# A recorded delta-rule kernel: loads of v and r on SyncE, transfers on fewer DMA engines, and other DMA costs in the planner of its order

## The chip, the core and the metric

The kernel runs on one core of a Trainium2 chip, with its five engines: TensorE (PE, whose weight loads the profile shows as PEld), VectorE (DVE), ScalarE (ACT), GpSimd (POOL) and SyncE (SP), and 16 DMA engines. Time is the device time of one execution in microseconds (us); the median of the runs is what is compared.

## The reference, cut to what matters

```python
def _attn_ref(r, k, v, w, a, b):            # each 4 x 8 x 768 x 40
    state = zeros((B, H, D, D))
    for t in range(S):
        y[:, :, t] = einsum('bhd,bhde->bhe', rt, state)
        Sa = einsum('bhde,bhe->bhd', state, at)
        state = state * wt[:, :, None, :] - einsum('bhd,bhe->bhde', Sa, bt)
        state = state + einsum('bhd,bhe->bhde', vt, kt)
    return y

def _moe_ref(x, w_skip, w_gate, w1, w2):    # x: 3072 x 320
    do_compute = x @ w_skip > 0
    xc = x[do_compute]
    e_idx = argmax(xc @ w_gate, axis=1)     # 8 experts, gate: softmax at e_idx
    for e in range(E):
        y[e_idx == e] = gate_w * (relu(xc[e_idx == e] @ w1[e]) @ w2[e])
    out[do_compute] = xc + y                # other rows: out = x
```

The first part is a recurrence over 768 steps for 32 heads with a decay w, a removal along a and b, and an added outer product of v and k. The second sends each of its 3072 rows with a positive skip score through one of 8 experts.

## The kernel before, in words

The 768 steps are cut into 24 chunks c of 32 steps; two chunks make a pair h of 64. The 32 heads lie in two halves x of 16. For each pair, VectorE turns the decay into running products (scan_z, scan_d, scan_w, on the tiles Z, D and Wx), kbm and l1a scale k, b and a by them, and m1 multiplies on TensorE to two matrices per head: one goes by ScalarE into AB, the other is transposed by VectorE, masked, and copied in four small transfers (32 rows of 256 numbers) into rows of L1. tinv inverts the triangular matrices of two pairs, step by step on VectorE (tinv0 for the first two pairs, in blocks of 16), into TB. kbt transposes k and b into L2, wex and wtt the decay into WT, m2 multiplies v by r and puts the result in R1.

Then each chunk goes through a chain: rs and ux multiply the state and the chunk's rows (R1) by L1, uq multiplies that by TB, GpSimd masks a part of it, sst makes the next state and yy the output, which VectorE scales into XS. SyncE stores XS to the output; route finds the expert of each row, and GpSimd scatters the rows by an indirect DMA into xg, which has been filled with padding (pad). When the chunks are done, experts runs the 8 experts over xg, with weights split into a high and a low part; load(e) brings the raw weights of expert e into WR, which holds KB and L1 of the first part until then.

The loads of the first part are: load_w (decay), load_kb (k and b), load_a (a), load_v (v as rows, 32 rows), load_rv (v, 64 or 128 rows, tiles vvt, SCR and one of rrt), load_rr (r, tiles rrt), l1z (zeros) and the identity rows idl. The first pairs are loaded in one piece of 104 or 128 rows, later ones in two pieces of 40 rows (cutl). Each takes the queue of the engine that issues it, in order: SyncE for most, and GpSimd for load_rv and load_rr behind the first chunk. In the built program, a transfer of SyncE also waits for the one that stands eight places ahead of it.

The order of all that is not the order of the code. Until chunk 22, the object Rec records every instruction as a task with its reads and writes. Rec.plan then goes through the tasks with costs for each engine (cost), for a transfer (pipe), for waits between engines (HOP, EX) and for TensorE's instruction stream (256 instructions to a block, a block at least BLK us), and takes on each engine the task with the smallest key, or a later one that is done within LET us of the other's start. flush issues the tasks in the order of their planned starts (line 272 in the profile). What stands behind chunk 22's flush keeps the order of the code (line 134). So a change of a cost moves instructions on all engines.

Of the kernel before, what the change touches and what calls it, by code (L numbers as in the profile page):

```python
# [15 lines left out]
DRAM = bass.MemoryType.DRAM  # L16
B,H,S,D=4,8,768,40
# [45 lines left out]
class Rec:  # L63
# [1 line left out]

    ENG=dict(vector='V',scalar='A',gpsimd='G',tensor='P',sync='S')
    HOP={'PA':0.066,'VA':0.034,'AV':0.033,'PV':0.11,'AP':0.053,'VP':0.055,'GP':0.054,'AG':0.08,'VG':0.13,'PG':0.17}
    EX=dict(V=0.08,P=0.07,A=0.0,G=0.0,S=0.0); PW=1.25; BLK=3.6; SLOW=0.8; BW=2.7e5; DSC=0.012; AHEAD=2.5
    def hop(s,e,f): return (0.114 if e=='V' else 0.0) if e==f else s.EX[e]+s.HOP.get(e+f,0.04)
    def __init__(s,nc):  # L70
        s.nc=nc; s.on=False; s.ni=0; s.tasks=[]; s.own={}; s.na=0; s.first={}; s.cache={}; s.banks={}; s.rest=()
# [28 lines left out]
    def cost(s,e,op,w,r,a):  # L100
        sz=lambda x: int(np.prod([d[1] for d in list(x.ap)[1:]])) if len(list(x.ap))>1 else 1
        n=max(sz(x) for x in (w[:1]+r[:1]))
        if 'dma' in op: return (1.06,2.6) if 'ind' in op else (0.63 if e=='S' else 0.55,2.2)
        ps=any('PSUM' in str(x.space).upper() for x in r)
        if e=='P':
            o=sz(w[0]); m=w[0].ap[0][1]
            if op=='transpose': return max(0.145,0.04+0.001*o),0
            if m<16: return 0.05+0.0016*o,0
            if m==16: return 0.022,0
            if m==32: return 0.034 if o<16 else 0.0098+0.00041*o,0  # L110
            if m<=48: return 0.0213+0.00072*o,0
            if m<=64: return max(0.072,0.028+0.00075*o),0
            return max(0.11,0.0021*o),0
        if e=='A': return 0.15+0.00085*n+(0.06+0.07*(n>99) if op=='activation' else 0.12 if abs(w[0].ap[-1][0])>8 and n>99 else 0.0),0
        if e=='G': return (0.08+n*0.0008 if op=='memset' else 0.18 if op=='tensor_copy' else 0.2+0.00195*n),0
        if op=='tensor_tensor_scan': return 0.02+0.00217*n,0
        if op=='transpose': return 0.08+0.00115*n*(1 if n<1000 else 1.6),0
        if op=='memset': return 0.04+0.0003*n,0
        if op=='reciprocal': return 0.17,0
        if op=='tensor_tensor': return (0.1 if ps and 'PSUM' not in str(w[0].space).upper() and n>199 else 0.06)+0.00105*n*(1 if ps or n<99 else 1.75),0  # L120
        return 0.12+0.00105*n,0
    def pipe(s,w,r):

        n=int(np.prod([d[1] for d in w.ap])); run=n
        for x in (w,r):
            q=1
            for st,k in reversed(list(x.ap)[0 if 'DRAM' in str(x.space).upper() else 1:]):
                if k>1 and st!=q: break
                q*=k
            run=min(run,q)  # L130
        p=w if 'DRAM' not in str(w.space).upper() else r
        return 4*n/min(6e5,5e3*max(16,p.ap[0][1]))+n/run*s.DSC/16
    def call(s,e,op,fn,a,k):
        if not s.on: return fn(*a,**k)  # L134
        def ap(x):
# [48 lines left out]
    def plan(s,keep=None):  # L184
# [33 lines left out]
        while done<N:  # L218
            best=None
            for e in 'VAGPS':  # L220
                c=[]
                for i in pool[e] if not keep else [i for i in pool[e] if i==seq[e][nxt[e]]]:
                    w=want(i) if T[i].al else (0.0,None)
# [15 lines left out]
            if e=='P':  # L239
                pos+=t.k  # L240
                while pos>=256*(blk+1):
                    x=max(fin[i],ent+s.BLK); fin[i]=x; ent=x; blk+=1
            if t.L and e in 'VG': port[e]=fin[i]
            free[e]=fin[i]; [pool[f].remove(i) for f in pool if i in pool[f]]; done+=1; nxt[e]+=1
            lat=t.lat
            if t.f==1: gi=fin[i]+s.IND
            elif e=='G' and t.f==2: gi=-1.0
            if t.x: dq=max(dq,fin[i]+1.0)+t.x; lat=max(lat+t.x,dq+1.2-fin[i])
            for j in t.n:
                rdy[j]=max(rdy[j],fin[i]+lat+s.hop(e,T[j].e)+(s.IHOP if T[j].f==1 and e=='V' else 0.0)); left[j]-=1  # L250
                if not left[j]: put(j)
# [2 lines left out]
                if not users[o]:  # L254
                    at[bank[o]]=last[o]
        s.st,s.fin,s.bank_of,s.en,s.span=st,fin,bank,en,max(fin)
    LET=0.7; FAR=1.0; ALT=1.0; FILL=None
    def keys(s):

        w=max(sum(t.d for t in s.tasks if t.e==e) for e in 'VAGP')/len(s.tasks)  # L260
# [44 lines left out]
def attn(ctx,tc,i,m,out,X):  # L305
# [10 lines left out]
    V,A,G,TE,SP=nc.vector,nc.scalar,nc.gpsimd,nc.tensor,nc.sync  # L316
# [32 lines left out]
    def load_kb(h):  # L349
        if h>=NH: return  # L350
        H[h]['KB']=KBa[h%4]; cutl(SP,H[h]['KB'],i['kb'][h],h<4,NK(h))
    def load_a(h,dst=None):
        if h>=NH: return
        H[h]['a']=a_.rearrange("p (u t) -> p u t",u=16) if dst is None else dst; cutl(SP,H[h]['a'],i['at'][h],h<5,PR)
    RR=[cp.tile([128,1024],F32,name=f"rrt{q}") for q in range(2)]; VV=[cp.tile([128,1024],F32,name="vvt"),SCR[:,0:1024]]
    rvt={}
    def load_rv(c,E=G):
        if c>=NC: return
        t=VV[0] if c%2==0 else RR[1] if c==1 else VV[1]
        rvt[c]=t.rearrange("p (u t) -> p u t",u=16); cutl(E,rvt[c],i['vv'][c],c<4,128)  # L360
    rrt={}
    def load_rr(h,E=G):

        if h>=NH: return
        rrt[h]=RR[h%2].rearrange("p (u t) -> p u t",u=16); cutl(E,rrt[h],i['rr'][h],h<2,128)
    def load_v(c,x):
        if c>=NC: return
        SP.dma_start(R1[x][c%NR1][ao[x]:ao[x]+32,:,0:40],i['vt'][c,x])
    def scan_z(h,dst=None,E=None,rv=rv):
        if h>=NH: return  # L370
        E=E or SE
# [32 lines left out]
        E.tensor_tensor(H[h]['KB'][0:NR(h),:,:,q,:],H[h]['KB'][0:NR(h),:,:,q,:],v4(Wi)[0:NR(h)],ALU.mult)  # L404
    def l1z(h,x):
        if h>=NH: return
        SP.dma_start(L1[x][h%NL][ao[x]:ao[x]+32].rearrange('p u c t -> p (u c t)'),i['zer'][0:32,0:1024])
    def l1a(h,x,E=None):
        if h>=NH: return
        E=E or G  # L410
# [208 lines left out]
    if 1:  # L619

        with tc.manual_schedule(engines={ET.Pool}):
# [15 lines left out]
            wchk(0,0); wchk(0,1)  # L637
            for x in range(2): zero(fR(x,0))
            for x in range(2): load_v(0,x)
            load_rv(0,SP); load_rr(0,SP); load_kb(2)  # L640
            scan_z(0,None,V); scan_d(0); scan_w(0,V); load_w(2)
            kbm(0,1); kbm(0,0,V); l1a(0,0,V); scan_z(1,alt[:,1041:2083],V); l1a(0,1,V)
            scan_d(1); scan_w(1,V)
# [4 lines left out]
            for x in range(2):  # L648
                for c in range(2): m1(0,x,c,V)
            for x in range(2): l1a(1,x,V)  # L650
            load_a(2,L1t[:,3072:4096].rearrange("p (u t) -> p u t",u=16)); load_rv(1,SP)
            for b in range(4): kbt(0,b)
            wchk(1,0); wchk(1,1)
            scan_z(2,None,V); scan_d(2); scan_w(2,V)
# [2 lines left out]
                for c in range(2): m1(1,x,c)  # L657
            for x in range(2): m2(0,x)
            for x in range(2):
                for c in range(2): SP.dma_start(L2[x][0][64*x:64*x+64,c],i['idl'][x,64*x:64*x+64])  # L660
            load_kb(3); load_w(3,alt[:,0:1041]); load_a(3,a1)
            t0=tinv0(Xi); next(t0)
            def Tb(k):
# [24 lines left out]
            load_a(4)  # L688
            wchk(3,0); wchk(3,1)
            for x in range(2):  # L690
                for c in range(2): SP.dma_start(L2[x][1][64*x:64*x+64,c],i['idl'][x,64*x:64*x+64])
        tg=iter(()); tn=[0]
        def T(k=1):
            tn[0]+=1
# [12 lines left out]
        for c in range(NC):  # L707
# [91 lines left out]
            if j==2: wex(2*ph+2,0)  # L799
            if c: m2(c+1,1)  # L800
            T()
            load_rv(c+2,G if c else SP)
            if c%2 or c==0: load_rr((c+3)//2,G if c else SP)
            if c<2: m.pad(2*c); m.pad(2*c+1)
            if c==22: m.load(1)
            RP('3c')
# [40 lines left out]
class Moe:  # L847
# [10 lines left out]
        s.base=s.base0; s.WH,s.WL={},{}  # L858
    def consts(s): s.nc.sync.dma_start(s.mc,s.i['mc']); s.nc.sync.dma_start(s.wg,s.i['wg'])
    def pad(s,k):  # L860
        s.nc.sync.dma_start(s.xg.rearrange("(q p) d -> p q d",p=128)[:,4*k:4*k+4],s.i['xpad'].unsqueeze(1).broadcast_to([128,4,XW]))
    def xpose(s,X):
        nc=s.nc
        pt=s.ps.tile([128,3,128],F32,tag="pp",name="ptx")
# [79 lines left out]
    def load(s,e):  # L944
        if e>=E_: return
        SP=s.nc.sync; r=s.raw[e%2]
        for k in range(2): SP.dma_start(r[:,1024*k:1024*k+1024],s.i['w1'][e,128*k:128*k+128])
        for k in range(2): SP.dma_start(r[64*k:64*k+64,2048:3072],s.i['w1'][e,256:320])
        for k in range(2): SP.dma_start(r[:,3072+1280*k:4352+1280*k].rearrange("p (k d) -> p k d",k=4),s.i['w2'][e,512*k:512*k+512].rearrange("(k p) d -> p k d",p=128))
    def base_last(s):  # L950
        s.nc.vector.tensor_copy(s.base1,s.base); s.base=s.base1
    def split(s,e,wp=None):
# [188 lines left out]
```

## Time and profile before

| | us |
|---|---|
| median of 3 runs (lowest, highest) | 624.01 (620.74, 625.52) |
| the profiled execution | 625.9 |
| its span, first to last instruction | 624.0 |
| busy in the span: PE, DVE, ACT, POOL | 470.0, 472.7, 390.0, 315.5 |
| mean granted clock of TensorE | 0.923 |

The span is what the trace covers; the profiled execution took 1.9 us more. Busy times are averages over stages of different kinds, so they are read by stretch. The DMA engines moved 80.59 MB, 129 GB/s over the span.

### The profile page before, as it was taken

Reading aid. Unit: us, or ns where it says so; the run is one execution under the profiler, and the core shown is the slowest. Engines: PE = TensorE matmul, PEld = TensorE weight load, DVE = VectorE, ACT = ScalarE, POOL = GpSimd, SP = SyncE. Lnnn points to the kernel's source line nnn. Section 1 sums busy time; section 2 is a strip of 40 time slices with the busy share of each in tenths; the row PEclk is TensorE's granted clock in tenths of the full one; section 3 lists DMA queues with packets and bytes.
Section 4 is the critical chain, followed back from the end, with each engine's and each line's share of the span. In section 5 each row is a group of like instructions: output and inputs, shape, how many; then the busy total and the mean of one; then the engine's idle time right before and its main releaser. Section 6 shows DMA issues by size and latency. Waiting matters only on the chain. (4 is left out here: it accounts for less than half of the span.)

```text
span 624.0 us, 28751 instructions
## 1 busy us (share of the span) xinstructions
PE 470.0 (75%) x12424; PEld 407.5 (65%) x12424; DVE 472.7 (76%) x1269; ACT 390.0 (62%) x982; POOL 315.5 (51%) x285
## 2 busy tenths in 40 slices
PE   0154327877787887887887789878977999999992
PEld 0143216666666666776776677667765799999992
DVE  6525894789997987998989879865783558898860
ACT  7073216878695877887696769577865455555510
POOL 4133626437491868477583853234223266666751
PEclk9997757899897998998798989989988999999997
DMA  8997232433452453425351534453663477775100
GB/s 190 251 270 226 78 99 65 130 81 92 93 137 75 108 143 100 133 67 147 87 153 40 144 98 109 101 153 95 167 168 93 123 220 232 240 225 156 43 18 18
DMA packets 64360, 80.59 MB, mean 129 GB/s; under 512 B 33698, under 2 KB 52719, under 8 KB 63124
## 3 DMA queue, kind: packets, MB, share of 16 engines
q1 hardware_dynamic: 58323, 64.55, 38.6%
q0 software_dynamic: 5904, 14.15, 8.2%
q8 instruction: 99, 1.62, 1.2%
q14 instruction: 34, 0.27, 0.1%
HBM read 67.80 MB, written 13.15 MB: 130 GB/s over the span
## 5 line engine op out<-in xcount | busy, mean ns | idle before, releaser
L272 ACT COPY R1t<-pc 32x288 f32<-32x288 f32 (+4 forms) x254 | 98.8, 389 | 38.1 <-PE pc L272 32.4
L272 POOL TENSOR_TENSOR R1t<-R1t,mc 64x512 f32<-64x512 f32 x43 | 55.5, 1292 | 70.9 <-ACT R1t L272 64.7
L272 DVE TENSOR_TENSOR px<-px,M 128x168 f32<-128x168 f32 (+10 forms) x240 | 61.2, 265 | 2.3
L134 POOL TENSOR_TENSOR WL<-WR,WH 128x1280 fp32r<-128x1280 f32 (+1 forms) x21 | 57.8, 2794 | 8.6 <-ACT WH L134 8.6
L272 POOL TENSOR_TENSOR WR<-WR,M 104x1024 f32<-104x1024 f32 x19 | 41.6, 2207 | 35.5 <-DVE M L272 22.9
L272 DVE TENSOR_TENSOR M<-M,px 128x168 f32<-128x168 f32 (+10 forms) x240 | 54.4, 255 | 2.0 <-DVE px L272 0.2
L272 DVE TENSOR_TENSOR_SCAN M<-M 104x1041 f32<-104x1041 f32 (+1 forms) x20 | 47.0, 2348 | 0.2
L272 ACT COPY R1t<-pq 32x256 f32<-32x256 f32 (+4 forms) x101 | 36.2, 358 | 8.4 <-PE pq L272 5.3
L134 ACT CAST WH<-WR 128x1024 fp32r<-128x1024 f32 (+1 forms) x35 | 39.6, 1132 | 0.0
L272 POOL DMA_INDIRECT xg<-XS,ix x20 | 24.1, 1206 | 29.9 <-DMA xg<-XS,ix 11.7
L134 POOL DMA_INDIRECT out<-ro,ti x16 | 15.8, 989 | 44.3 <-DVE ro L134 10.7
L272 PE MATMUL pc<-UX,TB 32*32 32x104 f32 (+1 forms) x1024 | 30.2, 245 | 9.0 <-issue 7.9
L134 ACT ACTIVATE hH<-pc 128x512 fp32r<-128x512 f32 x21 | 12.6, 599 | 37.8 <-PE pc L134 37.8
L134 DVE CAST ti<-xe 128x2 int32<-128x2 f32 x8 | 35.0, 4376 | 0.2
L272 PE MATMUL py<-L2t,R1t 128*32 128x40 f32 x1344 | 23.4, 208 | 12.1 <-issue 9.4
L134 PE MATMUL pc<-xH,WH 128*128 128x256 f32 x126 | 32.5, 283 | 0.0
L272 DVE TENSOR_TENSOR R1t<-pc,D 40x512 f32<-40x512 f32 (+1 forms) x44 | 26.6, 605 | 6.3 <-PE pc L272 4.2
L134 DVE TENSOR_TENSOR WL<-WR,WH 128x1024 fp32r<-128x1024 f32 (+1 forms) x19 | 23.8, 1253 | 9.9 <-ACT WH L134 9.4
L272 ACT COPY R1t<-ps 40x288 f32<-40x288 f32 (+4 forms) x72 | 27.5, 383 | 5.4 <-PE ps L272 4.2
L272 PE MATMUL ps<-R1t,L2t 128*40 128x72 f32 (+1 forms) x672 | 28.6, 233 | 2.8 <-ACT R1t L272 1.6
L272 PEld LDWEIGHTS pc<-UX,TB 32*32 32x32 f32 x1024 | 21.5, 107 | 14.0 <-issue 10.1
L272 PEld LDWEIGHTS py<-L2t,R1t 128*32 128x32 f32 x1344 | 17.7, 114 | 16.3 <-issue 11.7
(353 smaller groups left out, 1537.0 us busy)
## 6 DMA issues: line engine op xcount, KB each, us to landing
WR<-w SPq DMA_DIRECT2D x16, 640.0 KB
WR<-w SPq DMA_DIRECT2D x16, 512.0 KB
WR<-kb SPq DMA_DIRECT2D x16, 320.0 KB
WR<-w SPq DMA_DIRECT2D x16, 256.0 KB
R1t<-vt SPq DMA_DIRECT2D x48, 80.0 KB
out<-XS SPq DMA_DIRECT2D x24, 160.0 KB
rrt<-rr POOLq DMA_DIRECT2D x20, 160.0 KB, 5.4
vvt<-vv POOLq DMA_DIRECT2D x20, 160.0 KB, 6.1
```

Source lines behind the costliest of these rows:

```text
L134: if not s.on: return fn(*a,**k)
L272: for fn,a,k,own in s.tasks[i].calls: (fn if s.en[i]==s.tasks[i].e else s.nc.vector.tensor_copy)(*[at(x,own) for x in a],**{n:at(x,own) fo ...
```

## The change

Three things change. All calls of load_rv and load_rr take SyncE's queue. The 32 rows of v, the zero rows, the identity rows, the padding of xg and the weights of experts 0 and 1 get an outermost dimension of 8 on the side of the memory, by which the transfer is shared out to 8 DMA engines; the weights of later experts get 16, as many as before. Loads of 40 rows, all on SyncE now, run on 10. And the planner has other costs: one pipe of 200 GB/s that transfers pass one after the other, 1.7 us to land, no fixed 2.2 us; a block of TensorE's instructions at 3.4 us; LET 1.2.

```diff
-    EX=dict(V=0.08,P=0.07,A=0.0,G=0.0,S=0.0); PW=1.25; BLK=3.6; SLOW=0.8; BW=2.7e5; DSC=0.012; AHEAD=2.5
+    EX=dict(V=0.08,P=0.07,A=0.0,G=0.0,S=0.0); PW=1.25; BLK=3.4; SLOW=0.0; BW=2.0e5; AHEAD=2.5; LAND=1.7
...
-        if 'dma' in op: return (1.06,2.6) if 'ind' in op else (0.63 if e=='S' else 0.55,2.2)
+        if 'dma' in op: return (1.06,2.6) if 'ind' in op else (0.63 if e=='S' else 0.55,0.0)
...
-        p=w if 'DRAM' not in str(w.space).upper() else r
-        return 4*n/min(6e5,5e3*max(16,p.ap[0][1]))+n/run*s.DSC/16
+        return max(4*n/s.BW,n/run*0.002)
...
-                    x=max(fin[i],ent+s.BLK); fin[i]=x; ent=x; blk+=1
+                    x=max(fin[i],ent+s.BLK+s.SLOW*min(8.0,max(0.0,dq-ent))); fin[i]=x; ent=x; blk+=1
...
-            if t.x: dq=max(dq,fin[i]+1.0)+t.x; lat=max(lat+t.x,dq+1.2-fin[i])
+            if t.x:
+                a=fin[i]+(0.5 if e=='S' else 1.5); b=max(dq,a); dq=b+t.x
+                if t.x<0.3: b=a+0.4*(b-a)
+                lat=b+t.x+s.LAND-fin[i]
...
-    LET=0.7; FAR=1.0; ALT=1.0; FILL=None
+    LET=1.2; FAR=1.0; ALT=1.0; FILL=None
...
-    def load_rv(c,E=G):
+    def load_rv(c,E=SP):
...
-    def load_rr(h,E=G):
+    def load_rr(h,E=SP):
...
-        SP.dma_start(R1[x][c%NR1][ao[x]:ao[x]+32,:,0:40],i['vt'][c,x])
+        SP.dma_start(R1[x][c%NR1][ao[x]:ao[x]+32,:,0:40],i['vt'][c,x].rearrange('(a b) u d -> a b u d',a=8))
...
-            load_rv(c+2,G if c else SP)
-            if c%2 or c==0: load_rr((c+3)//2,G if c else SP)
+            load_rv(c+2)
+            if c%2 or c==0: load_rr((c+3)//2)
...
+        n=8 if e<2 else 16
-        for k in range(2): SP.dma_start(r[:,1024*k:1024*k+1024],s.i['w1'][e,128*k:128*k+128])
+        for k in range(2): SP.dma_start(r[:,1024*k:1024*k+1024],s.i['w1'][e,128*k:128*k+128].rearrange('(a b) f -> a b f',a=n))
```

The new order differs from the first rows on. On TensorE, at the start of the program, rrt with vvt or with the other rrt is m2, WR with mc is kbt, WE with mc is wtt, and WR 32x64 is m1. Before:

```order
L272 MATMUL pq_99<-mc,WE_130 128x104 x4
L272 MATMUL pc_101<-rrt_118,vvt 64x64 x8
L272 MATMUL pq_99<-rrt_118,vvt 64x64 x8
L272 MATMUL pc_100<-mc,WE_130 128x104 x4
L272 MATMUL pq_99<-rrt_118,rrt_119 64x32 x8
L272 MATMUL pc_100<-rrt_118,rrt_119 64x32 x8
L272 MATMUL pc_101<-mc,WR 128x104 x4
L272 MATMUL pq_99<-mc,WR 128x104 x4
L272 MATMUL pc_100<-WR 32x64 x16
```

On TensorE, the same place in the new order:

```order
L274 MATMUL pq_99<-mc,WE_130 128x104 x4
L274 MATMUL pc_101<-mc,WR 128x104 x4
L274 MATMUL pc_100<-mc,WR 128x104 x4
L274 MATMUL pq_99<-WR 32x64 x16
L274 MATMUL pc_101<-WR 32x64 x16
L274 MATMUL ps_103<-WR 32x64 x16
L274 MATMUL pc_100<-WR 32x64 x16
L274 MATMUL ps_102<-mc,WR 128x104 x8
```

The four rows of m2 have moved behind kbt and m1 of the first pairs; the first of them now stands 14 rows further down.

On VectorE, behind the two scans of pair 0 (M<-M), the scans of pair 1 (L2t) and the copies of token numbers from mc into XS. Before:

```order
L272 SCALAR_TENSOR_TENSOR M<-M 104x1040
L272 COPY XS_149<-mc 128x2
L272 MEMSET M 128x17
L272 COPY XS_150<-mc 128x2
L272 SCALAR_TENSOR_TENSOR L2t<-L2t,M 104x1041
```

On VectorE, the same place in the new order:

```order
L274 SCALAR_TENSOR_TENSOR M<-M 104x1040
L274 MEMSET M 128x17
L274 SCALAR_TENSOR_TENSOR L2t<-L2t,M 104x1041
L274 TENSOR_SCALAR D_125<-L2t 104x16
L274 RECIPROCAL M<-D_125 104x16
```

The copies into XS have moved 28 rows down, into the first steps of the inverse.

On SyncE, in the middle of the program, a piece of the new order with the loads that GpSimd issued before (vvt, SCR and rrt):

```order
L274 DMA out<-XS_149 4x32x320
L274 DMA vvt<-vv 40x1024 x2
L274 DMA M<-at 40x1024
L274 DMA R1t<-vt 32x16x40 x2
L274 DMA out<-XS_149 4x32x320
L274 DMA SCR<-vv 40x1024 x2
L274 DMA rrt_119<-rr 40x1024
L274 DMA L1t<-zer 32x1024
L274 DMA rrt_119<-rr 40x1024
L274 DMA L1t<-M 32x256
```

The loads of v and r now stand between the other transfers of a chunk, with zero rows, v rows and the small copies of m1 behind them. At the start of SyncE's order, M<-wt of pair 2 has moved ahead of mc, and the four transfers of padding have moved from the 22nd to 28th row to the 34th to 47th.

## Rows read from the trace of the kernel before

**Rows 1.** Table of stretches: length, busy us by engine, TensorE clock, DMA share, GB/s.

```profile
0.00:20.00 20.00, 0.00 (x0) 0.00 (x0) 9.74 (x11) 12.03 (x16) 7.14 (x11) 1.00 0.87 193
20.00:40.00 20.00, 4.12 (x47) 3.45 (x48) 12.84 (x13) 6.36 (x16) 2.15 (x1) 1.00 0.94 263
40.00:60.00 20.00, 11.45 (x322) 9.89 (x320) 7.22 (x10) 11.58 (x38) 9.92 (x6) 0.84 0.89 262
60.00:100.00 40.00, 14.60 (x630) 12.31 (x631) 32.85 (x62) 9.81 (x29) 18.30 (x27) 0.59 0.29 82
100.00:490.00 390.00, 318.02 (x10501) 260.78 (x10497) 318.65 (x1068) 289.89 (x803) 204.34 (x204) 0.94 0.43 111
490.00:590.00 100.00, 99.94 (x775) 99.47 (x776) 78.86 (x92) 54.77 (x74) 60.99 (x30) 1.00 0.64 190
```

**Rows 2.** Chain that ended last, its first piece: start, length, what.

```profile
475.11 0.07 DVE XS L134
```

**Rows 3.** VectorE in order of time, 0 to 60 us; idle before in brackets.

```profile
9.39 2.32 DVE L272 TENSOR_TENSOR_SCAN M<-M 104x1040 f32<-104x1040 f32 x1
22.40 0.25 DVE L272 COPY XS<-mc 128x2 f32<-128x2 f32 x2 [10.68 <-DMA mc<-mc]
...
35.43 0.07 DVE L272 MEMSET M<- 128x17 f32 x1
46.49 0.32 DVE L272 STREAM_TRANSPOSE M<-pc 128x128 f32<-128x128 f32 x1 [10.99 <-ACT M L272]
...
53.12 0.24 DVE L272 RECIPROCAL M<-D 104x16 f32<-104x16 f32 x1
59.08 1.25 DVE L272 STREAM_TRANSPOSE M<-M 128x1024 f32<-128x1024 f32 x1 [5.72 <-ACT M L272]
```

**Rows 4.** TensorE in order of time, 0 to 60 us.

```profile
22.51 0.93 PE L272 MATMUL pq<-mc,WE 104*128 104x104 f32 x4 [22.51 <-DMA mc<-mc]
30.26 1.12 PE L272 MATMUL pc<-rrt,vvt 128*64 128x64 f32 x16 [6.83 <-DMA rrt<-rr]
...
39.66 1.07 PE L272 MATMUL pq<-rrt,rrt 128*64 128x32 f32 x16 [6.54 <-DMA rrt<-vv]
...
41.52 0.96 PE L272 MATMUL pc<-mc,WR 104*128 104x104 f32 x4
...
57.87 0.69 PE L272 MATMUL pc<-WR,M 128*32 128x64 f32 x17 [3.84 <-issue]
```

**Rows 5.** DMA issues: out, in, queue, count, size of each.

```profile
xg<-xpad SPq DMA_DIRECT2D x4, 644.0 KB
...
L2t<-idl SPq DMA_DIRECT2D x8, 160.0 KB
...
M<-wt SPq DMA_DIRECT2D x2, 422.9 KB
```

**Rows 6.** Instructions on tile vvt: ns min/median/max, first and last start.

```profile
L272 POOL DMA_DIRECT2D vvt<-vv x20: 507/554/607, 116.9 to 425.7; - x20
L272 SPq DMA_DIRECT2D vvt<-vv x2: 339/346/352, 7.9 to 39.6; - x2
```

**Rows 7.** Waits of GpSimd, 100 to 490 us: us in total, times, longest.

```profile
POOL SCR L272 <- PE pc L272: 9.1, 3, 4.1
...
POOL vvt L272 <- PE pc L272: 6.2, 3, 4.6
...
POOL SCR L272 <- PE pq L272: 4.6, 2, 3.6
```

**Rows 8.** Waits of TensorE, 100 to 490 us, those without a releaser.

```profile
PE pc L272 <- issue: 12.1, 13, 3.8
...
PE py L272 <- issue: 9.4, 8, 3.2
PE pq L272 <- issue: 4.2, 7, 1.4
```

**Rows 9.** DMA queues, 100 to 490 us: packets, MB, share of 16 engines.

```profile
q8 instruction: 82, 1.34, 1.6%
```

More of the change, by code (lines that the diff above doesn't have):

```diff
@@ L406, in l1z @@
         if h>=NH: return
-        SP.dma_start(L1[x][h%NL][ao[x]:ao[x]+32].rearrange('p u c t -> p (u c t)'),i['zer'][0:32,0:1024])
+        SP.dma_start(L1[x][h%NL][ao[x]:ao[x]+32].rearrange('p u c t -> p (u c t)'),i['zer'][0:32,0:1024].rearrange('(a b) f -> a b f',a=8))
     def l1a(h,x,E=None):
@@ L639, in attn @@
             for x in range(2): load_v(0,x)
-            load_rv(0,SP); load_rr(0,SP); load_kb(2)
+            load_rv(0); load_rr(0); load_kb(2)
             scan_z(0,None,V); scan_d(0); scan_w(0,V); load_w(2)
@@ L650, in attn @@
             for x in range(2): l1a(1,x,V)
-            load_a(2,L1t[:,3072:4096].rearrange("p (u t) -> p u t",u=16)); load_rv(1,SP)
+            load_a(2,L1t[:,3072:4096].rearrange("p (u t) -> p u t",u=16)); load_rv(1)
             for b in range(4): kbt(0,b)
@@ L659, in attn @@
             for x in range(2):
-                for c in range(2): SP.dma_start(L2[x][0][64*x:64*x+64,c],i['idl'][x,64*x:64*x+64])
+                for c in range(2): SP.dma_start(L2[x][0][64*x:64*x+64,c],i['idl'][x,64*x:64*x+64].rearrange('(a b) u d -> a b u d',a=8))
             load_kb(3); load_w(3,alt[:,0:1041]); load_a(3,a1)
@@ L690, in attn @@
             for x in range(2):
-                for c in range(2): SP.dma_start(L2[x][1][64*x:64*x+64,c],i['idl'][x,64*x:64*x+64])
+                for c in range(2): SP.dma_start(L2[x][1][64*x:64*x+64,c],i['idl'][x,64*x:64*x+64].rearrange('(a b) u d -> a b u d',a=8))
         tg=iter(()); tn=[0]
@@ L860, in pad @@
     def pad(s,k):
-        s.nc.sync.dma_start(s.xg.rearrange("(q p) d -> p q d",p=128)[:,4*k:4*k+4],s.i['xpad'].unsqueeze(1).broadcast_to([128,4,XW]))
+        s.nc.sync.dma_start(s.xg.rearrange("(q p) d -> p q d",p=128)[:,4*k:4*k+4],s.i['xpad'].rearrange('(a b) d -> a b d',a=8).unsqueeze(2).broadcast_to([8,16,4,XW]))
     def xpose(s,X):
@@ L946, in load @@
         SP=s.nc.sync; r=s.raw[e%2]
-        for k in range(2): SP.dma_start(r[:,1024*k:1024*k+1024],s.i['w1'][e,128*k:128*k+128])
-        for k in range(2): SP.dma_start(r[64*k:64*k+64,2048:3072],s.i['w1'][e,256:320])
-        for k in range(2): SP.dma_start(r[:,3072+1280*k:4352+1280*k].rearrange("p (k d) -> p k d",k=4),s.i['w2'][e,512*k:512*k+512].rearrange("(k p) d -> p k d",p=128))
+        n=8 if e<2 else 16
+        for k in range(2): SP.dma_start(r[:,1024*k:1024*k+1024],s.i['w1'][e,128*k:128*k+128].rearrange('(a b) f -> a b f',a=n))
+        for k in range(2): SP.dma_start(r[64*k:64*k+64,2048:3072],s.i['w1'][e,256:320].rearrange('(a b) f -> a b f',a=n))
+        for k in range(2): SP.dma_start(r[:,3072+1280*k:4352+1280*k].rearrange("p (k d) -> p k d",k=4),s.i['w2'][e,512*k:512*k+512].rearrange("(k a b) d -> a b k d",k=4,a=n))
     def base_last(s):
```

## Prediction

> **What bounds the kernel now.** I read the table of stretches first, since the share of busy time over the whole span mixes stages with different limits [rows 1]. Four stages stand out. Up to 60 us the DMA engines are 87 to 94% busy at 193 to 263 GB/s while VectorE works only half of the first 40 us: this is the filling stage. From 60 to 100 us VectorE is busy 32.85 of 40 us and TensorE is at a granted clock of 0.59, so VectorE sets the pace there (the first triangular inverse). From 100 to 490 us, the 23 repeated chunks, VectorE is busy 318.65 of 390 us (82%) and TensorE 318.02, with DMA at 0.43: no one engine is full, and chains between the two set the pace. From 490 to 590 us TensorE is busy 99.94 of 100 us: the experts. The chain that ended last is of no help for the early stages: its first piece starts at 475.11 us [rows 2], so what happens before must be read from the waits.
>
> The second view is VectorE's instructions in order of time up to 60 us [rows 3]. It has three holes. After the scan at 9.39 us (2.32 us long, so until 11.71) it waits 10.68 us: the next instruction in its order copies a constant out of mc into XS, and mc has not landed. At 35.50 us it waits 10.99 us for ScalarE's copies of m1's products. At 53.36 us it waits 5.72 us for the last of them. In between and behind, its work follows back to back.
>
> The third view is TensorE over the same time, which tells why m1 is late [rows 4]. Its first product waits for mc until 22.51 us. The next waits 6.83 us for the first rr, a later one 6.54 us for the second v load, which lies in rrt; only at 41.52 us do the transposes of kbt(0) start, then m1. These waits are for loads that m1 does not read: TensorE runs in order, and m2's products stand in front of kbt and m1. The hole at 54.03 to 57.87 us (3.84 us) has no releaser but "issue".
>
> **The change part by part.** *The order at the start.* In the new order the two copies from mc stand behind the first triangular steps on VectorE, and on TensorE m2(0) stands behind kbt(0) and all of m1(0) and m1(1). I work out when VectorE would get m1's first product. (a) The 10.68 us hole goes: the scan of pair 1 needs only its own decay, which is an early load. (b) Behind it VectorE has the work that took from 22.40 to 35.50 us, 13.1 us, and ends at 11.71 + 13.1 = 24.8. (c) mc now stands behind one more load, M<-wt of 422.9 KB [rows 5], which at 193 GB/s [rows 1] is 2.2 us: mc lands at 22.5 + 2.2 = 24.7. TensorE's first product takes 0.93 us, so kbt(0) starts at 25.6. (d) From kbt's start to VectorE's first transpose of an m1 product passed 46.49 - 41.52 = 4.97 us; at the same pace that is 30.6 us. So the second hole is 30.6 - 24.8 = 5.8 us where it was 10.99, a gain of 5.2. (e) The third hole hangs on the 3.84 us at TensorE without a releaser; I keep it. The triangular inverse then starts at 59.08 - 10.7 - 5.2 = 43.2 us. What is late next: the inverse needs m1(2), which stands behind m2(1) and so behind the second v load; that load stands ten rows behind mc in SyncE's new order, with some 9 MB up to it, 45 to 50 us at 200 GB/s, and VectorE has the first steps of the inverse to do before it needs m1(2). Term: **-15.9 us**. If the later loads hold the inverse up, half of it stays (-8); if the third hole goes too, it is -21.6.
>
> *Loads of v and r move from GpSimd to SyncE.* GpSimd issues a v load in 554 ns, SyncE in 346 [rows 6]. GpSimd's time is not on the path (204 of 390 us busy [rows 1]), so what it gains costs or gives nothing by itself; the cover is its idle half. On SyncE each of these loads may wait for its buffer, and what is queued behind it are the v rows, the zero rows and the small copies of m1's triangles, which TensorE reads. The waits of GpSimd's queue for exactly this were 9.1 + 6.2 + 4.6 = 19.9 us in the three largest rows [rows 7]. The new order mixes these loads with the others at the places where their buffers come free, so I take 0 here and keep the 19.9 for a rival.
>
> *Fewer DMA engines per transfer, and TensorE's instructions.* Between 100 and 490 us TensorE was idle 12.1 + 9.4 + 4.2 = 25.7 us with no releaser but "issue" [rows 8], and queue q8 carried 82 packets of instructions, 1.34 MB [rows 9], which is 16 KB each; TensorE and its weight loads ran 20,998 instructions there [rows 1], 256 for each packet. So q8 is TensorE's instruction stream, and a block of it must land for each 256 instructions. It shares the DMA engines with the loads. No row tells which of them carries it. If it is one that the 8 and 10 lowest-numbered leave free, blocks come sooner. Bounds: 0 (the same engines, or the idle time is not from blocks) and -25.7. A shorter idle of TensorE shortens the span only where VectorE isn't busy, 18% of this stage: 25.7 x 0.18 = 4.6. Term: **-5 us**, with -12 and +4 as its ends (+4 because the whole order of this stage is new and may fit a little worse).
>
> The Trainium skill (Runtime: NRT & Kernel Launch, Instruction fetch mechanics) says that an engine streams its next block of 256 instructions while it runs the current one, so that crossing a block is mostly hidden. By that rule this term would be 0 and the sum 5 us higher; the rows with "issue" speak against it, since TensorE does stand still.
>
> *Loads of 8 engines that stay long.* From [rows 1], 263 GB/s at a share of 0.94 of 16 engines is 17.5 GB/s for one, 140 GB/s for eight. The identity rows (8 x 160 KB) and the padding of xg (4 x 644 KB) [rows 5] are 3.9 MB, some 28 us on eight engines where 16 would take 14. In the new order the padding stands behind the loads that the inverse needs, and nothing reads it until the first scatter, so I put them at 0. The weights of experts 0 and 1 are also issued long before the experts start.
>
> The experts from 490 us on keep their code, and TensorE is full there: 0.
>
> **The sum.** The profiled execution took 625.9 us (span 624.0 and 1.9 around it), 1.9 above the median of 624.01. 625.9 - 15.9 - 5 = 605.0, and on the scale of the median **603 us**.
>
> **The rivals.** *The instructions gain nothing.* Blocks travel on the engines that the loads use, or VectorE covers the idle time. Then only the start counts: 624 - 15.9 = 608. For it: DMA's share is only 0.43 in the middle, and VectorE is busy 82%. Against it: the rows of "issue".
>
> *The narrow pipe gives the start back.* With 8 engines at 140 GB/s the identity rows, the padding and whatever stands behind them on the same engines take 14 us more, and the triangular stage waits for loads in place of mc: 624 - 15.9 + 14 - 2 = 620, no difference that can be told. The Trainium skill (DMA: Bandwidth & Descriptors, Rules for kernel authors) says to use all 16 engines by keeping a dimension of a multiple of 16 outermost; this change does the opposite, and that rule stands behind this rival. For it: the first 60 us are full of DMA. Against it: from 60 to 100 us the share is 0.29, and the padding has no early reader.
>
> *SyncE's queue holds up the chunks.* Some 60 more loads at 0.35 us are 21 us of issue, and 19.9 us of waits move with them, ahead of v rows and small copies that each chunk reads. If all of that lands on the path it costs 41 us: 624 - 20.9 + 41 = 644; it beats the gain once half of it does, and with three quarters the time is 634, slower. For it: SyncE's queue is in order and every transfer of a chunk now passes it. Against it: with so little DMA traffic the loads have a chunk's time (390 / 23 = 17 us) to spare.
>
> **How the numbers follow.** A measurement of this kernel can tell about 1%, 6 us, from no change. Forecast (both terms, 603, own range 594 to 612): 0.55. Start alone (608): 0.23; also faster than 617.8. Narrow pipe (620): 0.12, no difference. SyncE's queue (634): 0.10, slower. So faster 0.78, same 0.12, slower 0.10. The lower end is the best of both terms, 624 - 21.6 - 10 = 592; the upper end takes in the narrow pipe, 620, and leaves out the 0.10 above and some 0.08 in the tails.
>
> **What the profile after would show.** Right: VectorE goes from its first pair of scans to the next without a wait for mc; its first transpose of an m1 product at about 31 us and the first large transpose of the inverse at 40 to 45 us, not 59.08; the first store of a chunk some 16 us earlier; TensorE's "issue" rows from 100 to 490 us clearly under 25.7 us; GpSimd without plain DMAs. Wrong: the start gains and the stretch of chunks gets longer by as much, with waits of TensorE for v, r or the small copies; or VectorE waits at the inverse for loads that stand late in the new order.

## The result, and the profile after

The changed kernel took 607.18 us at the median of four runs (603.48 to 613.85), beside 624.21 us for the kernel before in the same batch: a ratio of 0.972 with the interval 0.965 to 0.978. In a later batch it was 607.79 beside 620.47, a ratio of 0.981 (0.971 to 0.992). A disturbed run is left out of a ratio, so that it can differ a little from that of the two medians. The forecast was 603 us in a range of 592 to 620. The execution that was profiled took 603.48 us, with a span of 601.6, and was the shortest of the four. The spans of the two traces differ by 22.4 us, the two medians by 17.0, so the traces show some 5 us more gain than the runs.

The table of stretches, with the columns of [rows 1], of the changed kernel:

```profile
0.00:20.00 20.00, 0.00 (x0) 0.00 (x0) 17.82 (x17) 11.90 (x16) 13.00 (x13) 1.00 0.80 204
20.00:40.00 20.00, 13.90 (x323) 12.55 (x324) 18.36 (x21) 13.74 (x40) 8.68 (x4) 0.83 0.79 227
40.00:60.00 20.00, 9.87 (x232) 7.86 (x230) 19.45 (x39) 10.47 (x32) 11.09 (x18) 0.65 0.61 152
60.00:100.00 40.00, 23.79 (x1012) 20.47 (x1013) 25.47 (x61) 19.04 (x54) 16.41 (x15) 0.67 0.72 187
100.00:490.00 390.00, 322.45 (x10076) 267.10 (x10072) 315.05 (x1037) 284.99 (x780) 178.62 (x143) 0.93 0.42 116
490.00:590.00 100.00, 100.00 (x769) 99.39 (x769) 82.42 (x91) 50.61 (x69) 62.23 (x31) 1.00 0.52 161
```

The first three rows hold the change. VectorE works 55.6 of the first 60 us instead of 29.8 [rows 1], and the loads that filled the first 60 us now reach to 100 us (share 0.72 instead of 0.29). From 100 to 490 us GpSimd does 25.7 us less, as expected of a queue that no longer issues loads; the other engines are as busy as before.

VectorE in order of time, with the idle time ahead of a row in brackets, in the place of [rows 3]:

```profile
9.38 2.33 DVE L274 TENSOR_TENSOR_SCAN M<-M 104x1040 f32<-104x1040 f32 x1
...
11.90 2.33 DVE L274 TENSOR_TENSOR_SCAN L2t<-L2t,M 104x1041 f32<-104x1041 f32 x1
...
28.87 0.29 DVE L274 STREAM_TRANSPOSE M<-pq 128x128 f32<-128x128 f32 x1
...
37.47 1.25 DVE L274 STREAM_TRANSPOSE M<-M 128x1024 f32<-128x1024 f32 x1 [0.58 <-ACT M L274]
```

The first two holes are gone, and 0.58 us of the third is left. The first transpose of an m1 product comes at 28.87 us instead of 46.49, the large transpose that begins the inverse at 37.47 instead of 59.08. TensorE over the same time, in the place of [rows 4]:

```profile
23.41 0.93 PE L274 MATMUL pq<-mc,WE 104*128 104x104 f32 x4 [23.41 <-DMA mc<-mc]
24.13 1.59 PE L274 MATMUL pc<-mc,WR 104*128 104x104 f32 x8
25.65 1.08 PE L274 MATMUL pq<-WR 128*32 128x64 f32 x32
...
33.31 1.08 PE L274 MATMUL pq<-WR 128*32 128x64 f32 x32 [1.41 <-issue]
...
38.45 0.91 PE L274 MATMUL pc<-rrt,vvt 128*64 128x64 f32 x16
```

kbt follows mc within a microsecond, m1 follows kbt, and m2 at 38.45 us waits for no load. To see how much of the 21.6 us at the inverse arrives at the chunks, I read the rows on XS: the stores of the 24 chunks, with the first and the last start at the end of the row. Of the kernel before:

```profile
L272 SPq DMA_DIRECT2D out<-XS x21: 585/610/843, 112.7 to 444.8; - x21
L134 SPq DMA_DIRECT2D out<-XS x3: 558/604/612, 462.4 to 480.7; - x3
```

And of the changed kernel:

```profile
L274 SPq DMA_DIRECT2D out<-XS x21: 588/610/662, 95.1 to 425.0; - x21
L133 SPq DMA_DIRECT2D out<-XS x3: 598/612/612, 443.4 to 462.3; - x3
```

The first store comes 17.6 us earlier, the last 18.4. Of the difference of the two spans, 22.4 us, the start gives 17.6, the chunks 0.8 and what follows the last store 4.0 (143.3 against 139.3).

TensorE's waits without a releaser from 100 to 490 us, in the place of [rows 8]:

```profile
PE pc L274 <- issue: 10.3, 11, 3.1
...
PE ps L274 <- issue: 4.6, 4, 3.1
...
PE pq L274 <- issue: 3.2, 7, 0.6
...
PE py L274 <- issue: 1.4, 4, 0.5
```

The three rows that the prediction added up, 25.7 us, are 14.9 now (the row on ps, 2.1 before, is 4.6), yet the chunks are no shorter. The experiments return to this.

### The profile page after: what moved, and what is told of

Its sections match the earlier page's. It is cut to its first block, busy times and chain, and to the rows that moved or that the text cites. A ratio compares the mean times of both kernels' runs of the same rounds, so it can differ in the third digit from the quotient of the medians.

```text
span 601.6 us, 28743 instructions
## 1 busy us (share of the span) xinstructions
PE 473.8 (79%) x12424; PEld 410.9 (68%) x12424; DVE 479.7 (80%) x1263; ACT 390.7 (65%) x988; POOL 292.0 (49%) x224
## 4 chain that ended last, share of the span: by engine, by line
PE 46%; DVE 23%; issue 12%; ACT 11%; DMA 6%; POOL 1%; SPq 1%; POOLq 0%; DVEq 0%; ACTq 0%
PE pc L274 13%; DVE M L274 8%; PE pq L274 7%; ACT R1t L274 7%; PE pc L133 7%; PE ps L274 7%; PE px L133 5%; PE ps L133 5%; DVE R1t L274 4%; DVE px L274 3%; DMA mc<-mc 2%; DVE L2t L274 2%; DMA out<-ro,ti 1%; PE py L274 1%; DMA rrt<-rr 1%
## 5 line engine op out<-in xcount | busy, mean ns | idle before, releaser
L274 POOL TENSOR_TENSOR R1t<-R1t,mc 64x512 f32<-64x512 f32 x43 | 63.4, 1473 | 107.2 <-ACT R1t L274 90.3
L274 ACT COPY R1t<-pc 32x416 f32<-32x416 f32 (+4 forms) x213 | 83.3, 391 | 21.0 <-PE pc L274 17.4
L274 ACT COPY R1t<-pq 32x416 f32<-32x416 f32 (+4 forms) x122 | 46.5, 381 | 12.1 <-PE pq L274 8.5
L274 PE MATMUL ps<-R1t,L2t 128*40 128x40 f32 (+1 forms) x816 | 34.1, 234 | 6.5 <-issue 3.4
L274 PEld LDWEIGHTS ps<-R1t,L2t 128*40 128x40 f32 x816 | 27.4, 132 | 11.0 <-issue 4.5
L274 ACT COPY R1t<-ps 40x288 f32<-40x288 f32 (+4 forms) x86 | 30.4, 354 | 6.3 <-PE ps L274 5.2
L133 PE MATMUL ps<-WH,hH 128*128 128x320 f32 x88 | 27.6, 314 | 0.0
L133 PE MATMUL pc<-xH,WL 128*128 128x256 f32 x126 | 27.3, 281 | 0.0
L133 PE MATMUL ps<-WL,hH 128*128 128x320 f32 x88 | 27.2, 309 | 0.0
L133 PE MATMUL ps<-WH,hL 128*128 128x320 f32 x88 | 27.2, 309 | 0.0
```

What stands on the lines that cost most here:

```text
L274: for fn,a,k,own in s.tasks[i].calls: (fn if s.en[i]==s.tasks[i].e else s.nc.vector.tensor_copy)(*[at(x,own) for x in a],**{n:at(x,own) fo ...
```

## The experiments

Four batches on four chips. The kernel before ran beside each, with medians of 612.0, 620.5, 620.5 and 616.8 us, so times are compared within a batch alone. One profile is one run: the table gives, for each trace, the start of the inverse, the first store, the time from the first store to the last, and the rest of the span. No trace of the kernel before was taken in the batch of e1_costs to e4_pool.

| kernel | inverse | first store | chunks | rest | median, that of before beside it | ratio (interval) |
|---|---|---|---|---|---|---|
| before, first trace | 59.08 | 112.7 | 368.0 | 143.3 | | |
| before, second trace | 59.00 | 112.3 | 366.4 | 146.2 | 626.8 (one run), 620.5 | |
| after, first trace | 37.47 | 95.1 | 367.2 | 139.3 | 607.2, 624.2 | 0.972 (0.965 to 0.978) |
| after, second trace | 37.05 | 94.2 | 370.3 | 142.8 | 607.8, 620.5 | 0.981 (0.971 to 0.992) |
| e1_costs | 36.84 | 96.8 | 364.3 | 144.2 | 610.4, 612.0 | none given |
| e2_oldcosts | 57.00 | 116.8 | 356.2 | 142.9 | 617.7, 612.0 | 1.013 (1.003 to 1.022) |
| e3_wide | 35.73 | 92.8 | 364.8 | 139.6 | 602.5, 612.0 | 0.988 (0.979 to 0.998) |
| e4_pool | 34.93 | 92.7 | 363.3 | 143.6 | 602.5, 612.0 | 0.985 (0.975 to 0.996) |
| f1_xs | 57.60 | 110.8 | 368.3 | 144.1 | 622.0, 620.5 | 1.002 (0.998 to 1.007) |
| f2_m2 | 54.10 | 116.2 | 362.5 | 145.8 | 625.6, 620.5 | 1.009 (1.005 to 1.014) |
| f12 | 54.59 | 117.3 | 359.1 | 144.2 | 625.6, 620.5 | 1.008 (1.003 to 1.013) |
| f3_loads | 42.53 | 111.0 | 360.3 | 144.7 | 620.9, 620.5 | 1.002 (0.998 to 1.007) |
| f4_checks | 37.80 | 112.2 | 365.2 | 144.1 | 623.1, 620.5 | 1.004 (1.000 to 1.009) |
| f5_queue | 37.47 | 104.2 | 357.7 | 145.0 | 615.2, 616.8 | 0.999 (0.994 to 1.005) |

### Which of the three parts: e1_costs to e4_pool

The change has three parts: the planner's costs, the queue of v and r, and the number of DMA engines. Theory A is the prediction's main term: the order at the start pays, and it comes from the costs. The rivals are that the queue pays (B), or that fewer engines leave TensorE's instructions a free way (C). Four kernels take the parts apart.

e1_costs is the kernel before with the costs alone:

```diff
-    ... BLK=3.6; SLOW=0.8; BW=2.7e5; DSC=0.012; AHEAD=2.5
+    ... BLK=3.4; SLOW=0.0; BW=2.0e5; AHEAD=2.5; LAND=1.7
...
-    LET=0.7; FAR=1.0; ALT=1.0; FILL=None
+    LET=1.2; FAR=1.0; ALT=1.0; FILL=None
```

with cost, pipe and the lines of plan as in the change.

> The kernel before with the planner's new costs alone: v and r loads stay on GpSimd's queue, transfers stay on 16 engines. On VectorE and TensorE the first 40 rows stand as in the changed kernel. Theory A (the order at the start is what pays): the large transpose of the inverse comes near 37 us and the first store of a chunk near 95 us instead of 112.7, so 624 - 17 = 607 us (604 to 611). Theory B (the queue move pays, since GpSimd no longer spends time on issuing): nothing of the gain is here, 620 to 628. Theory C (fewer engines leave the instruction blocks of TensorE a free way): the start is earlier but what it costs in the middle stays, 609 to 613.

Measured: the start is that of the changed kernel (inverse 36.84, first store 96.8). The time does not decide: 610.4 at the median, 603.4 to 615.9, beside 612.0 (606.9 to 622.3). The times expected here and for the next three were worked out from 624 us; where the kernel before takes 612, only the ratio can be held against them.

e2_oldcosts is the changed kernel with these lines turned back.

> The changed kernel with the planner's old costs: v and r loads from SyncE's queue and fewer engines, but the order counts the old pipe. The start on VectorE has the copies of mc ahead of the scan of L2t again. Theory A: the hole of some 11 us on VectorE is back, the first store near 113 us, 624 us (619 to 628). Theory B: 607 to 612. Theory C: 617 to 620, with less issue time of TensorE between 100 and 490 us than the 25.7 us of the kernel before.

Measured: the start is back at the old place (inverse 57.00, first store 116.8), and the kernel is 1.3% slower than before (0.3 to 2.2%). So the queue and the fewer engines alone are no gain, and B falls. C falls with it: the kernel isn't faster though its engines are as few, and though TensorE's waits without a releaser are fewer, as C had expected (17.4 us in the chunks). The chunks are short, 356.2 us; but TensorE has 9,899 instructions between these stores instead of 9,994, and 1,520 ahead of the first instead of 1,424, so that part of the chunks' work is done ahead of it.

e3_wide is the changed kernel without its rearranges, as in

```diff
-        SP.dma_start(R1[x][c%NR1][ao[x]:ao[x]+32,:,0:40],i['vt'][c,x].rearrange('(a b) u d -> a b u d',a=8))
+        SP.dma_start(R1[x][c%NR1][ao[x]:ao[x]+32,:,0:40],i['vt'][c,x])
```

and the same for zeros, identity, padding and weights. Each engine keeps the very order of the changed kernel.

> The changed kernel with all its transfers on 16 engines again; the order of each engine's instructions is the very one of the changed kernel. Theory A: 607 us, no difference over 1%. Theory C: 610 to 613, and the time that TensorE waits for nothing shown (issue) in the chunks grows from 22.5 us by 4 or more.

Measured: 602.5 us, 1.2% under the kernel before of its batch (0.2 to 2.1%) and 15.1 us under e2_oldcosts, on the same chip; mc lands at 23.10 us, where the changed kernel has 23.41 and 22.99. With 8 engines or 16 the start is much the same.

e4_pool is the changed kernel with the loads of v and r on GpSimd (E=G again); its order is that of e1_costs, from which it differs in the number of engines alone.

> The changed kernel with the v and r loads back on GpSimd's queue; the order of each engine is that of the first kernel of this batch, which differs from it only in the transfers' engines. Theory A: as that one, 604 to 611. Theory B: 620 or more. Theory C: 3 to 5 us under the first one of this batch.

Measured: 602.5, beside 610.4 for e1_costs; mc lands at 22.43 us instead of 24.64. The runs overlap (600.7 to 609.8 and 603.4 to 615.9; the three shorter ones are 600.7, 601.4 and 603.5, the two shorter ones of e1_costs 603.4 and 607.1), and the pair of e3_wide and the changed kernel, never in one batch, shows nothing of the kind. What fewer engines are worth stays open within 1%. What is shown is that the costs are needed: with the old ones the start is late and nothing is gained (e2_oldcosts), and with the new ones either of the other two parts can be left out (e3_wide, e4_pool).

TensorE's waits without a releaser, added up over the rows from the first store to the last, are 28.6 and 21.4 us in the two traces of the kernel before, 21.0 and 24.2 in those of the changed kernel, 34.1 and 31.4 in e1_costs and e4_pool, 22.5 in e3_wide, 17.4 in e2_oldcosts. Two traces of one kernel differ by 7 us, and the chunks' length does not follow the sum: 368.0 and 366.4 us in these two, 364.3 at the largest sum. Between 16 and 8 engines in one order there is no step: 22.5 against 21.0 and 24.2, 34.1 against 31.4.

### The prediction's two moves by hand: f1_xs, f2_m2, f12

The prediction traced the start to two instructions out of place: copies of mc on VectorE (hole 1), m2 on TensorE (hole 2). By hand the planned start of just these tasks is raised in the kernel before, after the planner is done; whatever reads their results follows them. Nothing else moves, on any engine.

```diff
         s.deps(); s.keys(); s.plan()
+        s.later(1,1)
...
+                if T[i].e=='V' and has(T[i].W,'XS') and has(T[i].R,'mc') and s.st[i]<20: mv[i]=44.235+0.001*len(mv)
...
+            p=[i for i in N if T[i].e=='P' and s.st[i]<40 and (has(T[i].R,'rrt') or has(T[i].R,'vvt'))]
+            for q,i in enumerate(sorted(p,key=lambda i:s.st[i])): mv[i]=40.371+0.001*q
```

f1_xs has the first move, f2_m2 the second, f12 both. The kernel before ran with a profile, too.

> The kernel before once more, for a trace from the chip of this batch. On the chip of the last batch it took 607 to 616 us instead of 621 to 626. Theory A: what is shorter is the start (mc lands before 22.5 us, and the inverse begins before 59 us); the chunks from the first store to the last take 368 us, and from there to the end 143 us, as in the first trace. Rival: the chunks run faster, by more than 4 us.

> The kernel before with one edit by hand: VectorE's two copies of mc stand behind the scan of the third piece instead of ahead of the scan of L2t; nothing else in any engine's order moves. The prediction's terms (a) and (d) as a chain: the hole of 10.68 us goes, but TensorE's products of r and v still stand ahead of the first products of kb, so that VectorE waits the longer in its second hole; its first transpose stays near 46.5 us, the first store near 112.7: 0 to 3 us faster than the kernel before. Rival (each hole is worth its own length): 8 to 11 us faster.

> The kernel before with the other edit by hand: TensorE's five products of r and v (with ScalarE's copies of them and the reloads of r and v that they release) stand behind the first two pieces' products; the copies of mc stay ahead. Chain of the terms: the hole of 10.68 us stays, and VectorE reaches its first transpose at 35.5 us as before, but finds it ready there instead of waiting to 46.5: 9 to 13 us faster. Rival (each hole is worth its own length as the prediction wrote the sum): (d) alone, 5 us faster.

> Both edits by hand, and nothing else: old queue, old transfers, old order everywhere behind the start. Theory A (the start is all that the change gains): the first transpose near 30 us, the first store at 92 to 98 us, and 15 to 20 us faster than the kernel before, as much as the whole change. Rival (the planner's new costs pay also in the chunks): clearly less than the change, 8 to 12 us.

Measured: the second trace of the kernel before repeats the first within 2 us in the start and in the chunks. Why this kernel took 612.0 us in the batch of e1_costs to e4_pool stays open: here it was as slow as at first. f1_xs does as the chain said, with nothing gained; VectorE only waits at another place:

```profile
45.99 0.32 DVE L273 STREAM_TRANSPOSE M<-pc 128x128 f32<-128x128 f32 x1 [18.91 <-ACT M L273]
```

f2_m2 and f12 miss all that I had expected: 0.9 and 0.8% slower, and the first transpose of f12 still at 45.58 us. TensorE is now ahead, and ScalarE holds it up. ScalarE of f12 in order of time, the rows with long waits:

```profile
33.34 0.72 ACT L273 ACTIVATE junk<-M,wc 104x512 bf16<-104x512 f32 x1 [9.15 <-DMA M<-wt]
...
44.34 0.72 ACT L273 ACTIVATE junk<-L2t,wc 104x512 bf16<-104x512 f32 x1 [6.12 <-DMA L2t<-wt]
...
45.18 0.37 ACT L273 COPY M<-pc 128x128 f32<-128x128 f32 x1
```

These are readings of the next two pieces' decay (wchk), and they stand ahead of the copies that VectorE waits for. While m2 held TensorE up they cost nothing: in the kernel before ScalarE was as late as TensorE.

### The links behind them: f3_loads, f4_checks, f5_queue

Theory D: the readings are the next link. f3_loads keeps both moves and sets the loads of wt ahead on SyncE's queue, as in the changed kernel; f4_checks leaves the loads and sets the readings behind the copies. Both also put the second piece's m2 behind the first inverse.

```diff
+            put(10.78,lambda t,x: t.e=='S' and 13.3<x<13.4)
+            put(18.131,lambda t,x: t.e=='S' and 21.0<x<21.2)
...
+            put(42.2,lambda t,x: t.e=='A' and has(t.W,'junk') and 18<x<21)
+            put(43.0,lambda t,x: t.e=='A' and has(t.W,'junk') and 26<x<29)
```

The first two lines are f3_loads (with the loads around them moved along), the last two f4_checks. In both, one of m2's products lands in a bank of TensorE's results ahead of the transpose of the second piece's last block there, so that this block holds other numbers; f5_queue does not change any.

> Both edits by hand again, and on SyncE's queue the loads of wt for the third and fourth piece stand ahead of mc and of v and r, as in the changed kernel; the product of the second piece's r and v moves behind the first inverse, since it waited 4.11 us for a reload there. ScalarE's order is not touched. Theory D (what took the place of the two holes is ScalarE, whose readings of wt (ACTIVATE into junk) waited 9.15 and 6.12 us for these loads ahead of the copies that VectorE needs): the first transpose near 29 us, the inverse near 40, the first store at 95 to 101, 11 to 18 us faster than the kernel before. Rival (the start has a further chain, or the chunks give the gain back): under 5 us.

> Both edits by hand, the loads left as in the kernel before, and ScalarE's readings of wt for the third and fourth piece stand behind its copies of the first two pieces' products. Theory D: the first transpose near 29 us though the loads of wt land at 33 and 44 us as before; the inverse near 40 us, behind VectorE's scan that needs the first of them; the first store at 96 to 104, 8 to 17 us faster. Rival (it is the landing of the loads itself that holds the start): the first transpose still near 45 us, no gain.

> The changed kernel once more, beside the two by hand on one chip. Theory A: 15 to 20 us faster than the kernel before, the first store near 95 us, the chunks 367 us, as in its first trace.

Measured: for the inverse D was right. It begins at 42.53 and 37.80 us, the latter as early as in the changed kernel; the first transpose comes at 33.60 us in f3_loads, later than expected, and at 28.84 in f4_checks. For the time it was wrong: the first store stays at 111.0 and 112.2 us, and neither kernel is faster. The 17 and 21 us are lost again behind the start of the inverse. TensorE of f4_checks:

```profile
57.28 2.15 PE L273 MATMUL ps<-R1t,WR 128*32 128x104 f32 x32 [10.87 <-DMA WR<-M]
```

It waits for the small copies of the transposed blocks (WR from M). Their rows on tile WR, from 25 to 65 us, with first and last start; f4_checks:

```profile
L273 SPq DMA_DIRECT2D WR<-M x8: 507/512/599, 42.8 to 58.0; - x8
```

and the changed kernel:

```profile
L274 SPq DMA_DIRECT2D WR<-M x8: 507/538/558, 32.9 to 38.6; - x8
```

In f4_checks they stand on SyncE's queue behind padding, fourth pieces of k and b, and identity rows, and the queue waits for transfers eight places ahead of them: from 42.7 to 58.6 us, 6.5 us for padding and 3.6 for pieces of k and b. In the changed kernel they stand ahead of these. The changed kernel, on the same chip, was 1.9% faster than before.

f5_queue adds this to f4_checks (and sets m2 one transpose later):

```diff
+        put(42.0,lambda t,x: t.e=='S' and (16.9<x<19.2 or 30.2<x<30.3))
+        put(55.6,lambda t,x: t.e=='S' and (19.2<x<20.9 or 31.7<x<31.8 or 33.4<x<33.5))
+        put(58.0,lambda t,x: t.e=='S' and (21.9<x<22.1 or 24.6<x<24.7))
+        put(66.0,lambda t,x: t.e=='S' and x<36 and has(t.W,'xg'))
```

> The kernel before it in this row of edits by hand (both edits, ScalarE's readings of wt late, the loads of wt as in the kernel before), and now also SyncE's queue at the start in the order of the changed kernel: the transfers from M and SCR into WR, M and L1t, by which the transposed blocks come to their rows, ahead of the padding of xg, of kb's fourth piece, of the next v and r and of the identity. The first products of r and v stand one transpose later; ScalarE, VectorE and GpSimd keep their order, the loads of v and r in the chunks stay on GpSimd's queue, and every transfer keeps its 16 engines. Theory E (each hole closed lets the next waiting thing through, and the last one is that these transfers were issued from 43 to 58 us, where the changed kernel issues them from 32 to 38): the first store at 94 to 101 us, and 12 to 19 us faster than the kernel before: the whole gain of the change out of the start alone. Rival (the start cannot be had without the planner's order of the rest): the first store later than 105 us, under 6 us faster.

Measured: half of it. The copies go out from 35.1 to 40.2 us and the first store comes at 104.2 us, 8 us earlier than before and 9 to 10 us later than in the changed kernel. The median time is no better, 615.2 against 616.8 (its profiled run, 608.7, was the shortest of ten). VectorE of f5_queue shows where most of the rest is:

```profile
37.47 1.18 DVE L273 STREAM_TRANSPOSE M<-M 128x1024 f32<-128x1024 f32 x1
...
52.83 0.32 DVE L273 STREAM_TRANSPOSE M<-ps 128x128 f32<-128x128 f32 x1 [9.94 <-ACT M L273]
```

The old order has the transposes of the third piece among the first steps of the inverse; VectorE waits 9.94 us for them. In the changed kernel the inverse goes on without them. TensorE's first products of the inverse, which follow VectorE's steps, in f5_queue:

```profile
69.69 0.78 PE L273 MATMUL ps<-M 32*16 32x16 f32 x64 [14.96 <-DVE M L273]
```

and in the changed kernel:

```profile
63.23 0.74 PE L274 MATMUL ps<-M 32*16 32x16 f32 x64 [7.68 <-DVE M L274]
```

So the inverse is 6.5 us late there, and 2.6 more are lost between these products and the first store. This fifth link was not tried; nor is it shown why the 8 us that f5_queue's trace has at its first store are not in its median.

## Why the prediction was right, and where its reasons were not

**The size of the start was right.** It was put at -15.9 us, with -21.6 as an end. The first store came 17.6 us earlier in one trace and 18.1 in the other, in line with the five traces with the new costs (92.7 to 96.8 us) against 112.3 and 112.7. Of its steps: (b) VectorE's work until its first transpose was put at an end of 24.8 us and ended at 28.8: the step was mis-sized, since its 13.1 us came from a stretch in which GpSimd had one product into WR (25.04 us, 2.15 long); now it has three. VectorE:

```profile
14.26 2.08 DVE L274 TENSOR_SCALAR D<-L2t 104x16 f32<-104x16 f32 x1
...
18.90 3.10 DVE L274 TENSOR_TENSOR WR<-WR,M 104x1024 f32<-104x1024 f32 x1
21.93 4.42 DVE L274 TENSOR_TENSOR WR<-M 64x1024 f32<-64x1024 f32 x2
```

and GpSimd:

```profile
12.81 3.35 POOL L274 TENSOR_TENSOR WR<-WR,M 104x1024 f32<-104x1024 f32 x1 [5.56 <-DMA WR<-kb]
...
17.08 6.94 POOL L274 TENSOR_TENSOR WR<-WR,L2t 104x1024 f32<-104x1024 f32 x2 [0.78 <-DMA WR<-kb]
```

In the kernel before these rows of VectorE took 0.17, 1.19 and 2.46 us. The first now ends 0.18 us after GpSimd's first product (16.16), the last 2.33 us after its third (24.02), so each takes about its usual time once GpSimd is done; the second trace has other rows longer (two scans of 4.20 and 3.94 us, beside products of GpSimd that start at 11.77 and 16.24) and ends at 28.5. (c) mc was put at 24.7 us, 2.2 late for the load ahead of it, and landed at 23.41 and 22.99, under 1 us late. (d) So the first transpose came at 28.87 us without a wait, not at 30.6 behind one of 5.8. (e) The third hole, which I kept, shrank from 5.72 to 0.58 us: the stop of 3.84 us, which cut m1's last product in two, isn't there in the new order; one of 1.41 us stands ahead of the first of these products. The inverse thus began at 37.47, not 43.2, which is the end of -21.6; 4.0 of these 21.6 us are lost again ahead of the first store. No term held that loss. That the -15.9 lies so near to the 17.6 at the first store is in part luck: (c), (d) and (e) came out better than put, (b) and what follows the inverse's start worse.

The medians do not give all of it back everywhere: the gain was 17.0 us in the first batch, 12.7 in the later one, and 9.5 for e3_wide, which has the same order. Why it differs isn't shown.

**The reason was incomplete.** "(a) The hole goes" and "(d) the gain of 5.2" treat each hole as the work of the instruction behind which it stands. By hand, the two moves give nothing (f12). Behind m2 waits ScalarE with its readings of wt; behind these the small copies on SyncE's queue; behind these the transposes among the steps of the inverse. The prediction saw the move of M<-wt ahead of mc, and booked it as a cost of 2.2 us; it is one of the two ways by which ScalarE comes free (f3_loads). The planner's order loosens all links at once. That all come from one wrong cost, loads that it thought to have landed much earlier than they did, is argued from e1_costs, which changes the costs together; no run changes one of them alone. That the sum came out right although the mechanism had further links is luck of a kind: (b) to (d) measured how soon VectorE and TensorE could go if nothing else held them, and in the new order no wait of VectorE there is longer than 0.58 us.

**The term of the middle failed.** It was put at -5 us (-12 to +4) for TensorE's waits without a releaser. The chunks took 368.0 and 366.4 us before, 367.2 and 370.3 after: nothing, within the spread of some 3 us. The step that failed is the first: the 25.7 us of [rows 8] were one trace's. The same rows in the second trace of the kernel before, again from 100 to 490 us:

```profile
PE pc L272 <- issue: 10.6, 18, 2.0
PE py L272 <- issue: 7.7, 5, 3.6
...
PE pq L272 <- issue: 1.5, 3, 0.8
```

That is 19.8 us, and over all such rows some 7 us less than in the first, so that the fall seen after is no larger than chance. And fewer engines do not lower them (e3_wide against the changed kernel). (The lower end, 592, takes 10 us for this term, whose end was 12.) That makes the rival "the instructions gain nothing", 608 us, the better account of the result of 607.2: start alone. The Trainium skill (Runtime: NRT & Kernel Launch, Instruction fetch mechanics) calls the crossing of a block mostly hidden. The traces agree in part: TensorE stands still with no releaser in every trace, 17 to 34 us in the chunks, but the chunks' length does not follow it.

**What follows the last store** was put at 0. It took 143.3 and 146.2 us in the two traces before and 139.3 and 142.8 in the two after. In both kernels the longer one goes with the lower granted clock of TensorE there (0.98 and 0.95 of full speed before, 0.99 and 0.96 after). e3_wide has 139.6 us at 0.99, the other kernels 142.9 to 145.8 at 0.95 to 0.98. How much of the difference is the clock's isn't shown; no run was made on it.

**The other rivals.** The narrow pipe did not give the start back: mc lands no later with 8 engines (22.43 to 23.41 us) than with 16 (23.10 and 24.64), and the loads reach to 100 us without a wait of the inverse for them. (The -2 in that rival's sum has no source.) The Trainium skill (DMA: Bandwidth & Descriptors, Rules for kernel authors) asks for all 16 engines. No run here shows a loss from 8 where the loads have time, nor a certain gain (602.5 against 610.4 us in one batch, with runs that overlap). SyncE's queue did not hold up the chunks: the loads of v take 338 ns there (346 expected), and the chunks are as long as before.

## What to carry to other kernels

A wait names the one that came last, not all that would have waited: ahead of pricing a hole that a move closes, go on through every engine of that chain, and ask of each what it would wait for next; the gain is only what the last of these links allows. Where a planner sets the order, costs nearer to the truth (here, as argued above, of how late loads land) can loosen at once several links of which none pays by itself. A row of stray waits from one trace is no term of a sum until a second trace of the same kernel shows it. And the time of a piece of work, taken from one place in the order, holds at another only if the same engines run beside it there.

## What the runs showed of the hardware that was not expected

One kernel in one batch spread over 2% and more: the kernel before from 608.5 to 623.3 us in one batch and 613.6 to 627.9 in another, and its median from 612.0 to 624.2 between batches. The chunks of kernels whose order differs from that of before only at the start took 357.7 to 368.3 us from trace to trace (before, f1_xs to f5_queue). The spans of the two traces of the changed kernel differ by 5.7 us (601.6 and 607.3). A difference of some 5 us between two single profiles of this kernel tells nothing.

A stop of TensorE for which the trace names no releaser need not be TensorE's own. The longest single one was 3.8 and 4.4 us in the two traces of the kernel before and 3.4 in both of the changed one, but 14.9 in f3_loads and 7.3 in f2_m2. For these two, other rows tell what it waited for. The row of f3_loads:

```profile
82.52 0.75 PE L273 MATMUL ps<-M 32*16 32x16 f32 x64 [14.92 <-issue]
```

The same row in f4_checks, where the trace names VectorE, whose steps of the inverse stand ahead of it:

```profile
83.77 0.74 PE L273 MATMUL ps<-M 32*16 32x16 f32 x64 [14.68 <-DVE M L273]
```

In f2_m2 the stop ends 0.09 us after VectorE has made WR, which the stopped row reads; VectorE and TensorE:

```profile
28.74 3.11 DVE L273 TENSOR_TENSOR WR<-WR,M 104x1024 f32<-104x1024 f32 x1
...
31.94 0.93 PE L273 MATMUL pc<-mc,WR 104*128 104x104 f32 x4 [7.33 <-issue]
```

The stop of 3.84 us in [rows 4] is of another kind: it falls inside a row of 32 products, 17 of which come behind it. What TensorE waited for there, the traces don't show.
